# A Fourier mixer and an FFN on one core: first input by channel halves, sums before the inverse transform on GpSimd, and the first three token pairs in two passes over the weights

## The chip, the cores and the metric

One core of one Trainium2 chip. The metric is the device time of the whole program in microseconds; before the change it is 2591.12 us, the median of three runs from 2589.38 to 2592.61 us.

## What is computed

The input `x` has 8 sequences of 3008 tokens with 256 channels. Each sequence goes through a real Fourier transform over the tokens, a product with a complex filter, and the inverse transform; then a feed-forward network (FFN) is applied to every one of the 24064 tokens.

```python
X = np.fft.rfft(x, axis=1)
F = (filt_r + 1j * filt_i)[None, :, :]
y = np.fft.irfft(X * F, n=x.shape[1], axis=1).astype(np.float32)
x = y.reshape(B * S, D)
h = x @ w_in                        # 256 -> 2048
g = h * (1.0 / (1.0 + np.exp(-h)))
return (g @ w_out).astype(np.float32)   # 2048 -> 256
```

The two weight matrices arrive as 64-bit floats. The program reads them as 32-bit words and turns them into fp32 on the chip.

## The kernel before

**Order of work.** The program is written out by hand; there is no scheduler. Each engine executes its own instructions in program order, so a wait holds up everything behind it on that engine. Sequence ("batch") 0 is transformed alone, in a prologue. After that the FFN runs as 384 steps: 8 batches, 2 halves of the tokens, 3 *pairs* of token groups per half, and 8 blocks `jp` of hidden units. The transform of batch b+1 is cut into pieces that are placed between the matmuls of the FFN steps of batch b (`put(step, round, piece)`, `plan`, `plan_rest`). A step has eight rounds.

**An FFN step.** `hidden(step)` (L676) computes two 128-wide blocks of hidden units for two groups of tokens with seven matmuls in place of eight (a Strassen-Winograd scheme with weight blocks A11, A12, S3, A22, S1, S2, S4 in `w_t`). They go to three PSUM regions: `px` is used by four of them in turn, each after ScalarE has copied the value before it out (L697, L704, L710); `pyz` holds two more. VectorE adds the copies to `pyz` (L700, L711, L719) and makes the combinations of `g` (L721, `finish` L724); ScalarE applies SiLU. `project` (L735) does the seven matmuls of the step before, interleaved one by one, into the accumulators `acc`, which run over all eight `jp` of a pair. At the last one `drain` (L760) copies `acc` out, on ScalarE and VectorE by turns, and GpSimd makes seven sums (L776). `tokens(pair)` (L666) makes the combinations of a pair's inputs on VectorE before its first step.

**Weights.** There are 16 blocks j of 128 hidden units, two for each `jp`. `load_weights` brings the words, `split_weights` (L864) and `round_weights` (L890) build the exponent and the mantissa with L877, L880, L893, L895 and L899 on VectorE and L879 and L881 on ScalarE; for j = 0, 2, 4 and 6 ScalarE does L886 and L887 in place of L895. `place_weights` (L902) multiplies the two into `w_t` (L908, two instructions), and `combine_weights` (L918) makes the four Winograd sums of a `jp`. Blocks 0 to 8 are converted in the prologue, 9 to 15 in steps 0 to 6 (L1067), while the first stage of batch 1 (`stage1`, 8 pieces at round 3 of steps 0 to 7, L589) stands in the same steps.

**Prologue of batch 0.** `idle(36)` (L966) multiplies tables to warm TensorE up. `load_first` (L278) brings x in three DMAs, by tokens. `stage1_first` (L291) transforms 16 channels at a time with two matmuls each, and VectorE transposes each of the 16 results (L300). `forward(g)` (L425), for six groups g of frequencies, is the second stage. `multiply` (L441) does four VectorE instructions per group, PSUM times filter; `add` (L461) sums the products on GpSimd for g = 0 and 1 (`by_gpsimd`). For the other four groups the sums are made by TensorE, as extra terms of `inverse_first` (L482) with sign-changed tables `minus` and `neg`. `rows_first` (L502) copies the result on ScalarE and writes it to DRAM (`d2`), `load_t4` (L526) reads it back in another layout, `stage3` (L536) is the last stage and evacuates y. The conversion of blocks 2 to 8 is spread between these.

Of the kernel before, what the change touches and what calls it, by code (L numbers as in the profile page):

```python
# [46 lines left out]
FP32 = mybir.dt.float32  # L47
# [16 lines left out]
CH = 256  # L64
# [103 lines left out]
def kernel(  # L168
# [96 lines left out]
    def spectral(b):  # L265
# [12 lines left out]
        def load_first():  # L278


            view = w_t.rearrange("p j c w n -> p (j c w n)")
            for at, n0, n in ((view[:, 0:3072], 0, 12), (view[:, 3072:6144], 12, 12),
                              (x_all.rearrange("p i a n -> p (i a n)"), 24, 8)):
                nc.sync.dma_start(out=at, in_=bass.AP(tensor=x.tensor, offset=x.offset + n0 * C,
                                                      ap=[[32 * C, 128], [1, n * C]]))
            xs[0] = view[:, 0:6144].rearrange("p (n c) -> p n c", c=C)
            xs[1] = x_all.rearrange("p i a n -> p (i a n)").rearrange("p (n c) -> p n c", c=C)
            us["t2"] = view[:, 6144:14336].rearrange("p (s c) -> p s c", c=C)
            return view

        def stage1_first(k, i):  # L291

            if i == 0:
                banks[k] = bank(b, f"pa_{b}_{k}").rearrange("p a c -> p (a c)").rearrange(
                    "p (n c) -> p n c", c=16)
            n0, n = ((0, 24), (24, 8))[i]
            nc.tensor.matmul(out=banks[k][:, n0:n0 + n], lhsT=wx_t, rhs=xs[i][0:96, :, 16 * k:16 * k + 16],
                             start=True, stop=True)
            if i == 1:
                nc.vector.transpose(out=us["t2"][:, :, 16 * k:16 * k + 16].rearrange("p s c -> p c s"),  # L300
                                    in_=banks.pop(k).rearrange("p n c -> p c n"))
# [139 lines left out]
        def multiply(g, k):  # L441
            if b == 0 and g == NG - 1:

                room = raws["first"].bitcast(FP32).rearrange("p (k i r c) -> p k i r c", k=2, i=2, r=2)
                z, pt = room[:, k, 0], room[:, k, 1]
            else:
                z = zpool.tile([128, 2, C], FP32, name=f"z_{b}_{g}_{k}", tag="z")
            if b == 0 and g == NG - 1:
                pass
            elif b == 0 and k == 1:  # L450
# [9 lines left out]
        def add(g, k):  # L460
            z, pt = prods[g][k]  # L461
            eng = nc.vector if b > 0 else nc.gpsimd
# [19 lines left out]
        def inverse_first(g):  # L482
# [3 lines left out]
            pairs = prods.pop(g)  # L486
            halves[g] = ps
            for h in range(2):
                table = e_t[:, g] if h == 0 else minus[g // 4][:, g % 4]
                terms = [(table[:, :, 0], 0, 0), (table[:, :, 1], 0, 1)]  # L490
                if g not in by_gpsimd:
                    terms += [(table[:, :, 1], 1, 0), (neg[h][:, g], 1, 1)]
                for t, (lhs, which, ri) in enumerate(terms):
                    for i in range(2):
                        rows = slice(64 * i, 64 * i + 64)
                        for k in range(2):

                            nc.tensor.matmul(out=ps[i][64 * k:64 * k + 64, h, :], lhsT=lhs[rows, k],
                                             rhs=pairs[k][which][rows, ri, :], start=(h == 0 and t == 0),
                                             stop=(t == len(terms) - 1), skip_group_check=True)  # L500

        def rows_first(g):  # L502
            for i, pool, tag in ((0, qpool, "q"), (1, opool, "o")):
                qt = pool.tile([128, 2, C], FP32, name=f"q_{b}_{g}_{i}", tag=tag)
                nc.scalar.copy(out=qt, in_=halves[g][i])
                a0 = 8 * g + 4 * i
                queue = nc.gpsimd if g == NG - 2 else nc.scalar
                queue.dma_start(out=d2[a0:a0 + 4].rearrange("a n h c -> (a n) h c"), in_=qt)
# [17 lines left out]
        def load_t4(g, first=0, last=2 * NS):  # L526
# [4 lines left out]
            for h in range(2):  # L531
                queue = nc.scalar if first == 32 and h == 1 else nc.sync
# [125 lines left out]

    def combine(eng, out, in0, in1, op):
        eng.tensor_tensor(out=out, in0=in0, in1=in1, op=op)  # L660
# [5 lines left out]
    def tokens(pair):  # L666

        n, yt = pairs[pair][3], channels(pair)
        t = typool.tile([128, 4, CH], FP32, name=f"ty_{pair}", tag="ty")
# [4 lines left out]
        ty[pair] = t  # L674

    def hidden(step):  # L676

        pair, jp = divmod(step, NJP)
        n, yt, t = pairs[pair][3], channels(pair), ty[pair]
# [55 lines left out]
    def project(step):  # L735

        pair, jp = divmod(step, NJP)
        n, g = pairs[pair][3], g_t.pop(step)
        if jp == 0:
            acc[pair] = {}  # L740
        last = jp == NJP - 1

        order = PROJECT
        if jp == 0 and step in joined:
            order = PROJECT[0:2] + PROJECT[3:5] + PROJECT[2:3] + PROJECT[5:]
        elif jp == 0:
            order = PROJECT[2:3] + PROJECT[0:2] + PROJECT[3:]
        for c, k, i, h in order:
            if i not in acc[pair]:
                acc[pair][i] = accps.tile([128, 2, 256], FP32, name=f"acc_{pair}_{i}", tag=f"a{i}")  # L750

            nc.tensor.matmul(out=acc[pair][i][:, h, 0:n], lhsT=w_t[:, jp, c, 1], rhs=g[:, k, 0:n],  # L752
                             start=(jp == 0 and h == 0), stop=last, skip_group_check=True)
            if last and (h == 1 or i == 3):
                drain(pair, i)
            yield

    results = {}

    def drain(pair, i):  # L760
        n = pairs[pair][3]

        if i == 0:
            results[pair] = spool.tile([128, 8, CH], FP32, name=f"s_{pair}", tag="s")
# [3 lines left out]
        if pair == len(pairs) - 1:  # L768
            return drain_last(pair, i, n, s, acc[pair])
        copy = v.tensor_copy if i % 2 else nc.scalar.copy  # L770
        if i < 3:
            copy(out=s[:, 2 * i:2 * i + 2, 0:n], in_=acc[pair][i][:, :, 0:n])  # L772
            return
        copy(out=s[:, 6, 0:n], in_=acc.pop(pair)[3][:, 0, 0:n])
        for o, a, b in ((2, 0, 2), (5, 0, 5), (3, 5, 3), (6, 3, 6), (0, 5, 1), (4, 0, 4), (1, 3, 1)):
            combine(gp, s[:, o, 0:n], s[:, a, 0:n], s[:, b, 0:n], ALU.add)  # L776
# [363 lines left out]
```

## Time and profile before

| stretch (us) | what | PE | DVE | ACT | POOL | PE clock | DMA share |
|---|---|---|---|---|---|---|---|
| 0 to 14.4 | warm-up, first loads | 10.34 | 4.51 | 5.45 | 0.79 | 1.00 | 0.88 |
| 14.4 to 32.3 | first stage, transposes | 14.40 | 14.34 | 0.04 | 0.00 | 0.98 | 0.86 |
| 32.3 to 62.0 | filter, inverse, weights | 28.65 | 25.91 | 16.28 | 11.52 | 0.95 | 0.87 |
| 62.0 to 80.5 | weights, last stage | 15.23 | 16.52 | 10.26 | 8.22 | 0.79 | 0.81 |
| 80.5 to 151.5 | FFN steps 0 to 8 | 70.16 | 52.41 | 37.69 | 16.13 | 0.96 | 0.41 |
| 151.5 to 251.5 | FFN steps 9 to 23 | 100.00 | 66.04 | 40.76 | 13.09 | 1.00 | 0.22 |
| 251.5 to 2589 | the other steps | 2329.11 | 1511.54 | 996.42 | 376.68 | 1.00 | 0.23 |

The columns PE to POOL are busy microseconds of TensorE, VectorE, ScalarE and GpSimd in the stretch; the PE clock is the share of full speed that TensorE was granted, and the DMA share is the mean busy share of the 16 DMA engines. A busy TensorE here includes warm-up matmuls and matmuls at half clock, so its share alone doesn't say that it does useful work. A step's start is the start of its first matmul `px<-y` on TensorE.

### The profile page before, as it was taken

What the parts mean: (1) busy time and instruction counts of PE and PEld (TensorE: products, weight loads), DVE (VectorE), ACT (ScalarE), POOL (GpSimd) and SP (SyncE); (2) the same over time, 40 slices, a digit from 0 to 9 for tenths busy, and PEclk for the clock granted to TensorE, in tenths of its full rate; (3) what the DMA queues carried; (4) which work ended last, traced back from release to release, by engine and by line L of the source; (5) the groups of instructions that cost most, each with busy time, mean ns of one, the idle gap of its engine ahead of it and who ended that gap; (6) DMA issues with size and microseconds to landing.
All of it is one profiled execution on the core that took longest, in us unless ns stands there. A gap on an engine that the chain in (4) does not pass through costs nothing.

```text
span 2589.2 us, 48332 instructions
## 1 busy us (share of the span) xinstructions
PE 2567.9 (99%) x18972; PEld 2196.3 (85%) x18972; DVE 1691.3 (65%) x3569; ACT 1106.9 (43%) x3014; POOL 426.4 (16%) x672
## 2 busy tenths in 40 slices
PE   8999999999999999999999999999999999999998
PEld 6788888888888888888888888888888888888987
DVE  7766666666666766666666676666666676555554
ACT  3544444444444444443444434444444444444443
POOL 2211211121112111211122111211121112101101
PEclk9899999999999999999999999999999999999999
DMA  8431232222222222222223222231233211210000
GB/s 281 145 82 48 65 80 70 60 61 74 62 63 60 77 66 55 72 68 67 62 62 88 54 66 58 79 72 54 64 75 74 63 47 27 59 25 15 9 17 16
DMA packets 200076, 171.07 MB, mean 66 GB/s; under 512 B 122116, under 2 KB 174196, under 8 KB 199060
## 3 DMA queue, kind: packets, MB, share of 16 engines
q1 hardware_dynamic: 178520, 117.04, 18.7%
q0 software_dynamic: 16928, 44.65, 5.3%
q10 hardware_dynamic: 4400, 6.29, 0.8%
q8 instruction: 149, 2.44, 0.4%
q14 instruction: 79, 0.65, 0.1%
HBM read 96.05 MB, written 81.26 MB: 68 GB/s over the span
## 4 chain that ended last, share of the span: by engine, by line
PE 95%; DVE 1%; DMA 1%; ACT 1%; issue 0%; SPq 0%; ACTq 0%; DVEq 0%
PE acc L752 43%; PE px L689 26%; PE pyz L689 19%; PE pd L547 3%; PE pb L433 2%; PE pc L476 2%; PE pf L403 1%; PE pa L340 0%; DMA w_t<-in_x_dram 0%; DVE g L660 0%; PE pa L331 0%; DMA filt<-in_filt_i_dram 0%; ACT t L344 0%; DMA e_t<-e_tbl 0%; DVE w_t L660 0%
## 5 line engine op out<-in xcount | busy, mean ns | idle before, releaser
L752 PE MATMUL acc<-g,w_t 128*128 128x256 f32 (+1 forms) x5376 | 1512.0, 375 | 0.4 <-DVE g L660 0.4
L752 PEld LDWEIGHTS acc<-g,w_t 128*128 128x128 f32 x5376 | 1021.3, 190 | 115.7 <-DVE g L660 0.8
L660 DVE TENSOR_TENSOR g<-pyz,abc 128x256 f32<-128x256 f32 (+1 forms) x1152 | 479.7, 416 | 563.0 <-ACT abc L710 325.0
L660 DVE TENSOR_TENSOR g<-g 128x256 f32<-128x256 f32 (+3 forms) x1152 | 609.9, 529 | 196.9 <-ACT g L693 183.7
L689 PE MATMUL px<-ty,w_t 128*128 128x256 f32 (+1 forms) x2304 | 684.4, 379 | 0.5 <-ACT abc L710 0.5
L693 ACT ACTIVATE g<-g 128x256 f32<-128x256 f32 (+1 forms) x1152 | 472.9, 410 | 246.7 <-DVE g L660 246.7
L689 PEld LDWEIGHTS px<-ty,w_t 128*128 128x128 f32 x2304 | 426.3, 190 | 82.3 <-issue 26.6
L660 POOL TENSOR_TENSOR s<-s 128x256 f32<-128x256 f32 (+1 forms) x329 | 257.1, 799 | 1439.1 <-DVE s L772 1377.4
L689 PE MATMUL pyz<-y,w_t 128*128 128x256 f32 (+1 forms) x1536 | 452.9, 377 | 0.0
L689 PEld LDWEIGHTS pyz<-y,w_t 128*128 128x128 f32 x1536 | 284.3, 189 | 44.8 <-DVE g L660 5.0
L704 ACT COPY abc<-px 128x256 f32<-128x256 f32 (+1 forms) x384 | 141.5, 368 | 361.3 <-PE px L689 361.3
L710 ACT COPY abc<-px 128x256 f32<-128x256 f32 (+1 forms) x384 | 143.1, 373 | 323.7 <-PE px L689 323.7
L693 ACT ACTIVATE g<-px 128x256 f32<-128x256 f32 (+1 forms) x384 | 146.1, 381 | 308.6 <-PE px L689 308.6
L689 PE MATMUL px<-y,w_t 128*128 128x256 f32 (+1 forms) x768 | 230.2, 381 | 1.1 <-ACT y L246 1.0
L689 PE MATMUL pyz<-ty,w_t 128*128 128x256 f32 (+1 forms) x768 | 225.7, 376 | 0.2 <-DVE g L660 0.2
L689 PEld LDWEIGHTS px<-y,w_t 128*128 128x128 f32 x768 | 141.9, 189 | 23.6 <-issue 5.9
L689 PEld LDWEIGHTS pyz<-ty,w_t 128*128 128x128 f32 x768 | 145.9, 190 | 17.4 <-DVE g L660 1.0
L697 ACT COPY abc<-px 128x256 f32<-128x256 f32 (+1 forms) x384 | 135.5, 353 | 19.5 <-PE px L689 19.5
L547 PEld LDWEIGHTS pd<-wi_t,t 48*64 48x64 f32 x4096 | 69.3, 139 | 32.0 <-ACT g L693 16.4
L547 PE MATMUL pd<-wi_t,t 48*64 48x47 f32 x4096 | 77.2, 238 | 2.3 <-DMA t<-d 1.9
L415 POOL DMA_DIRECT2D d<-tf x144 | 71.4, 503 | 24.0 <-DVE tf L411 20.4
L772 ACT COPY s<-acc 128x512 f32<-128x512 f32 (+1 forms) x94 | 54.3, 578 | 47.5 <-PE acc L752 47.5
(114 smaller groups left out, 1309.1 us busy)
## 6 DMA issues: line engine op xcount, KB each, us to landing
t<-d SPq DMA_DIRECT2D x120, 192.0 KB
d<-q POOLq DMA_DIRECT2D x86, 256.0 KB, 2.6
t<-d SPq DMA_DIRECT2D x84, 256.0 KB
out_dram<-o SPq DMA_DIRECT2D x636, 32.0 KB
d<-tf POOLq DMA_DIRECT2D x144, 96.0 KB, 3.0
xr<-in_x_dram SPq DMA_DIRECT2D x6, 1472.0 KB
x_all<-in_x_dram SPq DMA_DIRECT2D x72, 96.0 KB
x_all<-xr SPq DMA_DIRECT2D x72, 96.0 KB
```

What stands on the lines that cost most here:

```text
L415: nc.gpsimd.dma_start(out=d1[k // 2, :, k % 2, n0:n0 + 4], in_=us["tf"][32 * k:32 * k + NS].rearrange("p q n c -> p (q n) c"))
L433: nc.tensor.matmul(out=ps[k][32 * j:32 * j + 32, ri, :], lhsT=d_t[rows, 4 * g + at, ri, :], rhs=t2[rows, at, :], start=True, stop=True)
L476: nc.tensor.matmul(out=ps[j][64 * k:64 * k + 64, a, :], lhsT=e_t[rows, g + a, k, ri, :], rhs=zs[k][rows, ri, :], start=(a == 0 and ri == 0 ...
L547: nc.tensor.matmul(out=ps[h][c0:c0 + 64, cb, i, :], lhsT=t4s[g][rows, i, 128 * cb + c0:128 * cb + c0 + 64], rhs=wi_t[rows, :], start=True, ...
L660: eng.tensor_tensor(out=out, in0=in0, in1=in1, op=op)
L689: nc.tensor.matmul(out=out, lhsT=w_t[:, jp, c, 0], rhs=rhs, start=start, stop=True, skip_group_check=True)
L693: nc.scalar.activation(out=g[:, k, 0:n], in_=g[:, k, 0:n] if src is None else src, func=AFT.Silu)
L697: nc.scalar.copy(out=sums[:, 0, 0:n], in_=xo)
L704: nc.scalar.copy(out=sums[:, 1, 0:n], in_=xo)
L710: nc.scalar.copy(out=sums[:, 2, 0:n], in_=xo)
L752: nc.tensor.matmul(out=acc[pair][i][:, h, 0:n], lhsT=w_t[:, jp, c, 1], rhs=g[:, k, 0:n], start=(jp == 0 and h == 0), stop=last, skip_group ...
L772: copy(out=s[:, 2 * i:2 * i + 2, 0:n], in_=acc[pair][i][:, :, 0:n])
```

## The change

It has five parts. (1) x of batch 0 comes as channels 0 to 127 in one DMA and channels 128 to 255 in two, on 96 partitions, in runs of 128 channels; the first eight transposes need the first DMA alone. (2) All sums before the inverse transform are made by GpSimd, except those of the second half of groups 4 and 5, which VectorE makes; the extra terms on TensorE and the `neg` tables are gone. (3) Only blocks 0 to 3 are converted before the FFN, blocks 1 to 3 after the inverse transform. Blocks 4 to 15 are converted in steps 0 to 3 and 5 to 12, and their Winograd sums are made by GpSimd. (4) So that the FFN can start with four blocks, pair 0 runs over `jp` 0 and 1, pairs 1 and 2 over `jp` 0 to 3, and each takes the rest later: six runs in the place of three, with three more `tokens`, three more drains and a partial sum that GpSimd adds. (5) Some queues change: `load_t4` of the last rows of groups 2 and 3 goes to ScalarE's queue, and several buffers are used for other things.

```diff
-            for at, n0, n in ((view[:, 0:3072], 0, 12), (view[:, 3072:6144], 12, 12),
-                              (x_all.rearrange("p i a n -> p (i a n)"), 24, 8)):
-                nc.sync.dma_start(out=at, in_=bass.AP(tensor=x.tensor, offset=x.offset + n0 * C,
-                                                      ap=[[32 * C, 128], [1, n * C]]))
+            for at, n0, n, c0 in ((view[:, 0:4096], 0, 32, 0), (view[:, 4096:6144], 0, 16, 128),
+                                  (x_all.rearrange("p i a n -> p (i a n)"), 16, 16, 128)):
+                at = at.rearrange("p (n c) -> p n c", c=128)
+                nc.sync.dma_start(out=at[0:96], in_=bass.AP(tensor=x.tensor, offset=x.offset + n0 * C + c0,
+                                                            ap=[[32 * C, 96], [C, n], [1, 128]]))
...
-            eng = nc.vector if b > 0 else nc.gpsimd
+            eng = nc.vector if b > 0 or (g > 3 and k == 1) else nc.gpsimd
...
-                if g not in by_gpsimd:
-                    terms += [(table[:, :, 1], 1, 0), (neg[h][:, g], 1, 1)]
...
-                nc.scalar.copy(out=qt, in_=halves[g][i])
+                copy = nc.vector.tensor_copy if (g, i) == (NG - 1, 1) else nc.scalar.copy
+                copy(out=qt, in_=halves[g][i])
...
-                queue = nc.scalar if first == 32 and h == 1 else nc.sync
+                queue = nc.scalar if first == 32 and g > 1 else nc.sync
...
+    runs = [(0, 0, 2), (1, 0, 4), (2, 0, 4), (0, 2, 8), (1, 4, 8), (2, 4, 8)]
+    runs += [(pair, 0, NJP) for pair in range(3, len(pairs))]
+    schedule = [(run, jp) for run, (_, first, end) in enumerate(runs) for jp in range(first, end)]
...
+        kept = partial.pop(pair, None)
+        if end < NJP:
+
+            room = x_all[:, pair - 1] if pair else upool.tile([128, 2, 512], FP32, name="partial", tag="u")
+            partial[pair] = room.rearrange("p a (i n) -> p (a i) n", n=CH)
         for o, a, b in ((2, 0, 2), (5, 0, 5), (3, 5, 3), (6, 3, 6), (0, 5, 1), (4, 0, 4), (1, 3, 1)):
...
+        if kept is not None:
+            for k, o in enumerate(FINAL):
+                combine(gp, s[:, o, 0:n], s[:, o, 0:n], kept[:, k, 0:n], ALU.add)
...
+    for g in range(4):
         part["forward"](g)
     for g in range(NG):
         for k in range(2):
             part["multiply"](g, k)
+            part["add"](g, k)
+        if g == 3:
+            part["forward"](5)
+        if g > 0:
+            inverse(g - 1)
+        if g == 1:
+            part["forward"](4)
...
+    inverse(NG - 1)
     for later in range(4):
+        part["load_t4"](later, 32, 2 * NS)
+    split(1)
+    rounded(1)
+    placed(1)
     combine_weights(0)
+    split(2, 3)
+    rounded(2, 3)
+    placed(2, 3, eng=gp)
+    combine_weights(1, eng=gp)
+    weights(6, 7)
+    idle(24)
     for g in range(4):
         part["stage3"](g)
...
-    for j in range(9, NJ):
-        put(j - 9, 1, lambda j=j: (split(j), rounded(j)))
-        put(j - 9, 5, placed, j)
+    for j in range(4, NJ):
+        at = j - 4 if j < 8 else j - 3
+        put(at, 1, lambda j=j: (split(j), rounded(j)))
+        put(at, 5, placed, j)
         if j % 2:
-            put(*((j - 8, 5) if j < 15 else (j - 9, 6)), combine_weights, j // 2, 0)
-            put(*{13: (j - 8, 7), 15: (j - 8, 1)}.get(j, (j - 7, 5)), combine_weights, j // 2, 1)
+            put(at + 1, 1, lambda jp=j // 2: combine_weights(jp, eng=gp))
...
+    begun = ((-2, 1), (0, 5), (4, 5), (8, 5), (14, 5), (18, 5))
...
+        step, rnd = begun[run] if pair < 3 else combines[pair % per]
+        pending.append((pair // per * STEPS + step + rnd / ROUNDS, 98, lambda run=run: tokens(run)))
```

## The prediction

> **What bounds the kernel now.** I read the page first: its busy shares, then its chain of work that ended last.
>
> ```profile
> PE 2567.9 (99%) x18972; PEld 2196.3 (85%) x18972; DVE 1691.3 (65%) x3569; ACT 1106.9 (43%) x3014; POOL 426.4 (16%) x672
> PE 95%; DVE 1%; DMA 1%; ACT 1%; issue 0%; SPq 0%; ACTq 0%; DVEq 0%
> ```
>
> TensorE sets the end, and the change leaves the FFN's matmuls as they are. So only two things can move the time: when FFN step 0 starts, and how long TensorE stalls in the steps whose VectorE and ScalarE work changes. The timeline of the prologue (start, duration, engine and line):
>
> ```profile
> 3.60 10.31 PE L964 MATMUL idle<-wx_t 96*128 96x128 f32 x72 [3.60 <-DMA wx_t<-wx_tbl]
> 17.95 14.25 DVE L300 STREAM_TRANSPOSE w_t<-pa 128x512 f32<-128x512 f32 x16 [7.25 <-PE pa L297]
> 34.33 0.69 DVE L455 TENSOR_TENSOR z<-pb,filt 128x512 f32<-128x512 f32 x1 [0.89 <-PE pb L433]
> 61.95 7.86 PE L964 MATMUL idle<-wx_t 96*128 96x128 f32 x68
> 72.10 6.76 PE L547 MATMUL pd<-wi_t,t 48*64 48x47 f32 x246 [1.89 <-DMA t<-d]
> 80.54 1.19 PE L689 MATMUL px<-y,w_t 128*128 128x256 f32 x2 [0.98 <-ACT y L246]
> ```
>
> Transposes run from 17.95 to 32.2, the filter products start at 34.33, the inverse ends at 61.95, the last stage at 79.6, and step 0 starts at 80.54. Then the timeline of a step that converts a block (the step that starts at 105.08), with one line from a later step without conversion:
>
> ```profile
> 107.98 0.42 DVE L877 TENSOR_SCALAR e<-raw 128x512 uint32<-128x512 uint32 x1
> 108.43 0.72 ACT L879 ACTIVATE e<-e,bias_t 128x512 f32<-128x512 uint32 x1 [1.96 <-DVE e L877]
> 109.06 0.61 ACT L881 ACTIVATE m<-m 128x512 f32<-128x512 uint32 x1
> 109.58 0.35 ACT L704 COPY abc<-px 128x256 f32<-128x256 f32 x1
> 109.71 0.69 DVE L893 SCALAR_TENSOR_TENSOR m<-raw,m 128x512 f32<-128x512 uint32 x1 [0.97 <-ACT m L881]
> 111.52 0.42 DVE L660 TENSOR_TENSOR g<-pyz,abc 128x256 f32<-128x256 f32 x1
> ...
> 147.82 0.37 ACT L704 COPY abc<-px 128x256 f32<-128x256 f32 x1 [0.94 <-PE px L689]
> ```
>
> The `px` copy L704 comes 4.50 us after the step's start, behind L879 and L881; in the step that starts at 145.39 without a conversion it comes after 2.43 us. TensorE doesn't feel it, because the first stage of batch 1 (four matmuls, 1.72 us) stands just there. Such steps last 7.84 to 7.97 us; 14 matmuls of 0.4315 us and 1.72 make 7.76.
>
> **What the skill says.** The Trainium skill, "SBUF — State Buffer", section "Who interferes with whom": a VectorE instruction with two SBUF inputs, or in a two-port mode, and a GpSimd instruction that reads SBUF exclude each other; one with a PSUM input doesn't. The trace agrees:
>
> ```profile
> 63.46 3.44 POOL L660 TENSOR_TENSOR w_t<-w_t 128x256 f32<-128x256 f32 x4 [0.47 <-DVE w_t L908]
> 63.63 0.95 DVE L880 TENSOR_SCALAR scratch<-raw 128x512 uint32<-128x512 uint32 x1
> 72.55 0.96 DVE L895 TENSOR_SCALAR e<-e 128x512 uint32<-128x512 f32 x1
> 74.68 1.71 DVE L908 TENSOR_TENSOR w_t<-m,e 128x256 f32<-128x256 f32 x2
> 153.55 1.49 DVE L660 TENSOR_TENSOR g<-g 128x256 f32<-128x256 f32 x2
> ```
>
> Beside GpSimd L880 takes 0.95 us for 0.42, L908 1.71 for 0.75, `finish` 1.49 for 0.87; L899 took 1.11 for 0.69; the products from PSUM stay at 0.68. "TensorE: Matmul & The Clock Gate", section "What's actually happening", says that about 3.4 us of idling halve the clock; the trace has 0.50 from about 73 to 86 us although TensorE waited just 1.9 us, so I assume half clock at the same place after. "DMA: Bandwidth & Descriptors", section "Specifications", gives 512 bytes as the least for line rate; the packets of 512 bytes in the trace have a median of 27 ns, 303 GB/s over 16 engines, against 460 ns for 12288 bytes (427 GB/s).
>
> **The prologue after.** *First input.* The first DMA has 3072 packets: 3072 x 27 ns / 16 = 5.2 us. With block 0 (some 1.5 us) and a start at 3.0 it lands near 10.5, the other two near 13 and 16. But `idle(36)` holds TensorE until 13.9, so the first result comes at 14.8, and transposes run from 15.0 to 29.2: 3.0 us are won, not seven. At twice the packet time the DMAs land near 15, 20 and 25.5; the last eight transposes (7.1 us) then end at 33.5, 1.3 us later than before. Filter products start at 34.33 - 3.0 = 31.3.
>
> *Filter and inverse.* VectorE has 24 products of 0.60 us without conversions between: 14.4 us. The GpSimd sums take 0.69 each (35.77 to 40.56), 2.75 per group against 2.4 for VectorE, and trail without holding it; buffers are free in time. VectorE's own four sums read SBUF beside GpSimd: 4 x 0.95 less overlap, some 3.5. The last sum is done at 49.2, the last inverse (1.9 us, as at 41.09 to 43.0) at 51.3: 10.6 us before 61.95.
>
> *Last stage.* Copy 0.6, two issues, 2.3 us from issue to the reader's start (50.36 to 52.72): rows are in DRAM near 55.5. Synchronous queue: 8 + 8 + 2 issues of 0.42 and one of 0.34 from 48.2 end at 56.1, with gaps 56.5; with 2.5 us to land (69.28 to 72.10 before, less the issue) `stage3` starts at 59.0 and, at 7.1 us as before, ends at 66.1. *Weights.* ScalarE is in order, and its four `load_t4` issues wait for those rows: until 57.2 nothing behind them runs, and L879 of block 1 is behind them. From there L879 and L881 1.25, L893 to L899 1.6, L908 0.75, sums of `jp` 0 1.5, four L877/L880 1.4, ScalarE's share of blocks 2 and 3 3.7, then its five y copies of 0.8: 57.2 + 14.2 with 1.0 of overlap = 70.4. This is later than TensorE's 66.1 + 1.2, so step 0 starts at 70.4: **-10.1 us** (bounds 67.5 and 73.5).
>
> **The FFN after.** Ideal step lengths are the same; I add stalls.
>
> *Conversions without the first stage beside them.* Blocks 11 to 15 fall in steps 8 to 12. There L704 still comes after about 4.65 us, so the fifth `px` matmul starts at 5.1, not 3.45: +1.65 us each in steps 8 and 9. In 10 and 11 `stage3` (1.26 us) fills most of it, but its y copies add 0.8; in 12 `forward` leaves 0.4: 1.65 x 2 + 0.8 x 2 + 0.4 = **5.3**.
>
> *GpSimd beside conversions.* The drains of the three first runs put seven sums (5.5 to 5.95 us) into steps 3, 7 and 11, which convert. `finish` (+0.6), L877, L880, L895 (+0.53 each) and L893, L899 (+0.42 each) give 3.0; 0.5 vanishes in the 0.97 us wait for L881. I take 2.0 each, bounds 1.0 and 2.5. Behind these wait L704, the fifth `px` matmul and all after it. Sums of `jp` 2 and 5 (2.9 to 3.9 us) cover `finish` in steps 2 and 9: 0.5 each. **7.0**, bounds 3 and 9.
>
> *More `tokens`.* 1.46 us each at round 5 of steps 0 and 8, ahead of L719 and the next step's `finish` and L877: the free time there is 1.1 to 1.4, L908 takes 0.75 of it: 1.3 + 1.1; the first `tokens`, beside GpSimd's sums of `jp` 1, +1.0: **3.4**. In step 4 it is hidden, as nothing is converted.
>
> *Drains and the rest.* ScalarE's copy of 0.59 before the next `px` copy: 0.45 in each of steps 2, 6 and 10; steps 13 to 18 +0.7; block 6 needs L886 and L887 on ScalarE, +1.3 in step 2: **3.4**. GpSimd's 12 sums of the partial results are read a step later: 0.
>
> *Removed.* The stalls of steps 1 to 7 before (7.84 + 7.89 + 7.85 + 7.97 + 7.85 + 8.65 + 7.98 by the starts of `px<-y`, less 7 x 7.76) are 1.7, 0.2 in step 8: **-1.9**.
>
> Sum: 5.3 + 7.0 + 3.4 + 3.4 - 1.9 = +17.2; with -10.1 it is +7.1, and 2591.1 + 7.1 = **2598 us**.
>
> **Rivals.** *A, no change:* the two engines' exclusion costs 3, `tokens` and drains half: 5.3 + 3 + 1.7 + 1.7 - 1.9 = 9.8 against -10.1: 2591. For it: most VectorE work of a step reads PSUM. Against: a conversion doesn't. *B, faster:* step 0 at 67.5 (TensorE's limit, if rows land earlier than under the load seen at 58 to 62) and stalls of 6, as if only the missing first stage counted: 2591 - 13 + 6 = 2584. For it: in the step at 105.19 VectorE is busy 6.25 of 7.86 us, so there is room on average; against: the order, not the busy time, sets L704. *C, first input late:* at 54 ns a packet transposes end 1.3 us later than before instead of 3.0 earlier, and tables and filters, which ScalarE issues after the second DMA has landed, some 2 us later still: 2598 + 6 = 2604. For it: packets of 1024 bytes rise from a median of 46 ns to 71 when two queues press on the engines at 28 to 32 us; against: at 3 to 16 us the DMA moves 415 GB/s.
>
> **How the numbers follow.** Forecast 0.47 (0.02 of it within 0.2%), A 0.20, B 0.23, C 0.10. The bound of 0.2% is 5.2 us: slower 0.45 + 0.10 = 0.55, same 0.22, faster 0.23. The low end, 2583, takes in the better half of B; with stalls at their bounds the forecast reaches 2591 to 2604, and part of C goes to 2606.
>
> **What would show it.** First transpose at 15.0; products of the last group end near 47; last inverse ends near 51; step 0 at 70.4, with ScalarE's L879 of block 1 behind its `load_t4` issues. Steps 8 and 9 at 7.7 us or more instead of 6.1; steps 3, 7 and 11 at least 1.5 us over their ideal. I am wrong if L879 of block 1 runs before the rows have landed, if step 0 comes before 68, or if steps 3 and 7 last under 8.3 us.

## The result and the profile after

The changed kernel takes 2617.45 us (2617.03 to 2618.9, 4 runs) against 2591.76 (2589.38 to 2592.61) for the kernel before in the same comparison: a ratio of 1.010, 95% interval 1.0085 to 1.0114, slower. The forecast was 2598 us, at most 2606. The direction was right, the size was not: +27.1 us between the two profiled spans (2616.3 and 2589.2) instead of +7.1.

The page of the kernel after, busy shares and chain of work that ended last:

```profile
PE 2564.7 (98%) x18792; PEld 2188.3 (84%) x18792; DVE 1708.9 (65%) x3573; ACT 1107.3 (42%) x3017; POOL 475.7 (18%) x732
PE 93%; DVE 3%; DMA 2%; ACT 1%; issue 1%; SPq 0%; ACTq 0%; DVEq 0%
```

TensorE's part of the chain falls from 95 to 93%, VectorE's rises from 1 to 3 and the DMA's from 1 to 2; GpSimd works 49 us more. So the places to look are the DMA in the prologue and VectorE in the FFN steps.

The timeline of the prologue after (start, duration, engine and line):

```profile
3.88 10.49 PEld L975 LDWEIGHTS idle<-wx_t 96*128 96x128 f32 x72 [3.88 <-DMA wx_t<-wx_tbl]
16.15 7.07 DVE L299 STREAM_TRANSPOSE w_t<-pa 128x512 f32<-128x512 f32 x8 [7.18 <-PE pa L297]
18.93 0.19 ACT L985 COPY warm<-w_t 96x1 f32<-96x1 f32 x1 [10.67 <-DMA w_t<-in_x_dram]
23.78 7.09 DVE L299 STREAM_TRANSPOSE w_t<-pa 128x512 f32<-128x512 f32 x8 [0.56 <-PE pa L297]
32.10 0.69 DVE L453 TENSOR_TENSOR z<-pb,filt 128x512 f32<-128x512 f32 x1 [0.67 <-PE pb L432]
38.54 1.76 ACT L995 ACTIVATE minus<-e_t,bias_t 128x1024 f32<-128x1024 f32 x2 [19.42 <-DMA filt<-in_filt_r_dram]
41.42 0.69 DVE L453 TENSOR_TENSOR room<-pb,filt 128x512 f32<-128x512 f32 x1 [4.45 <-DMA filt<-in_filt_i_dram]
67.58 0.72 ACT L890 ACTIVATE scratch<-scratch,bias_t 128x512 f32<-128x512 uint32 x1 [8.56 <-DMA t<-d]
72.32 7.39 PE L542 MATMUL pd<-wi_t,t 48*64 48x47 f32 x256 [11.06 <-DMA t<-d]
80.68 0.76 PE L691 MATMUL px<-y,w_t 128*128 128x256 f32 x1 [0.97 <-ACT y L246]
```

FFN step 0 starts at 80.68 us, where it started at 80.54 before: the prologue won nothing, though it converts four weight blocks instead of nine. The second DMA of the input has landed only at 18.93 (14.25 before), and with it everything that ScalarE issues behind it is late: `minus` at 38.54, a filter product that waits 4.45 us for its filter. L890 of block 1 (the prediction's L879) sits behind the `load_t4` issues as forecast, but until 67.6 us, not 57.2.

The timeline of FFN step 9 after (it converts block 12):

```profile
164.22 3.65 POOL L660 TENSOR_TENSOR w_t<-w_t 128x256 f32<-128x256 f32 x4 [7.20 <-DVE w_t L919]
165.82 1.47 DVE L660 TENSOR_TENSOR g<-g 128x240 f32<-128x240 f32 x2
167.21 0.94 DVE L888 TENSOR_SCALAR e<-raw 128x512 uint32<-128x512 uint32 x1
168.19 0.72 ACT L890 ACTIVATE e<-e,bias_t 128x512 f32<-128x512 uint32 x1 [3.05 <-DVE e L888]
168.82 0.61 ACT L892 ACTIVATE m<-m 128x512 f32<-128x512 uint32 x1
169.34 0.34 ACT L706 COPY abc<-px 128x240 f32<-128x240 f32 x1
169.73 1.17 PE L691 MATMUL px<-ty,w_t 128*128 128x240 f32 x2 [2.52 <-ACT abc L706]
170.69 1.81 PE L755 MATMUL acc<-g,w_t 128*128 128x240 f32 x4
```

Read it from the top: GpSimd's four Winograd sums of `jp` 5 run from 164.22 to 167.87. Beside them `finish` takes 1.47 us and L888 0.94 instead of 0.42. ScalarE's L890 waits for L888, L706 stands behind L890 and L892, and TensorE waits 2.52 us for L706. The last two lines are new: after the wait two matmuls take 1.17 us where they take 0.57 otherwise, because the granted clock there is 0.50. Such a step before had no wait of TensorE for L706 at all.

By the starts of `px<-y`, steps 0 to 23 take 197.3 us after and 170.9 before, 26.4 more. From step 24 on the two traces differ by 0.6 us in 2338. So the prologue gave 0.1 us, these FFN steps 26.4 and the rest 0.6.

### The profile page after: what moved, and what is told of

Same layout as the page of the kernel before. It is cut to its first block, busy times and chain, and to the rows that moved or that the text cites. A ratio compares the mean times of both kernels' runs of the same rounds, so it can differ in the third digit from the quotient of the medians.

```text
span 2616.3 us, 48075 instructions
## 1 busy us (share of the span) xinstructions
PE 2564.7 (98%) x18792; PEld 2188.3 (84%) x18792; DVE 1708.9 (65%) x3573; ACT 1107.3 (42%) x3017; POOL 475.7 (18%) x732
## 3 DMA queue, kind: packets, MB, share of 16 engines
q1 hardware_dynamic: 184280, 115.99, 18.7%
## 4 chain that ended last, share of the span: by engine, by line
PE 93%; DVE 3%; DMA 2%; ACT 1%; issue 1%; SPq 0%; ACTq 0%; DVEq 0%
PE acc L755 42%; PE px L691 25%; PE pyz L691 18%; PE pd L542 3%; PE pb L432 2%; PE pc L474 2%; DVE g L660 1%; PE pf L402 1%; DMA w_t<-in_x_dram 1%; DMA d<-q 1%; PE pa L339 0%; DMA t<-d 0%; DMA d_t<-d_tbl 0%; DVE e L888 0%; DVE ty L660 0%
## 5 line engine op out<-in xcount | busy, mean ns | idle before, releaser
L660 DVE TENSOR_TENSOR g<-g 128x256 f32<-128x256 f32 (+3 forms) x1152 | 616.6, 535 | 196.8 <-ACT g L695 183.6
L691 PE MATMUL px<-ty,w_t 128*128 128x256 f32 (+1 forms) x2304 | 686.7, 380 | 13.3 <-ACT abc L706 11.3
L660 POOL TENSOR_TENSOR s<-s 128x256 f32<-128x256 f32 (+1 forms) x338 | 264.8, 800 | 1427.5 <-DVE s L777 1372.6
L706 ACT COPY abc<-px 128x256 f32<-128x256 f32 (+1 forms) x384 | 141.4, 368 | 356.5 <-PE px L691 356.5
```

Source lines behind the costliest of these rows:

```text
L691: nc.tensor.matmul(out=out, lhsT=w_t[:, jp, c, 0], rhs=rhs, start=start, stop=True, skip_group_check=True)
L706: nc.scalar.copy(out=sums[:, 1, 0:n], in_=xo)
```

## The experiments

All kernels are the kernel after with the edit shown, unless said otherwise. FFN step 0 at 80.68 us and the step lengths of the kernel after are the yardstick: steps 2, 3, 7, 9 and 11 take 12.15, 9.68, 10.69, 11.06 and 11.77 us, 55.4 together.

### First input: packet size or partitions?

`x_tokens128` reads the first input again by tokens, `x_tokens96` does so into the 96 partitions that are used:

```diff
-  for at, n0, n, c0 in (... two channel halves, [[32 * C, 96], [C, n], [1, 128]])
+  for at, n0, n in ((view[:, 0:3072], 0, 12), (view[:, 3072:6144], 12, 12), (x_all..., 24, 8)):
+      nc.sync.dma_start(out=at[0:P], in_=... ap=[[32 * C, P], [1, n * C]])      # P = 128 or 96
   # (stage1_first is that of the kernel before)
```

> The kernel after, with the first input read as in the kernel before (three DMAs by tokens on 128 partitions, packets of 12288 bytes instead of 512). Theory T1: the 512-byte packets (46 ns each, some 200 GB/s) hold the DMA engines until about 22 us and push filters, tables and weight loads back into the time of the d2 writes. Then here the last transposes end at 32 us as before, minus is made at 33 instead of 38.5, the last inverse ends at 51 to 53 instead of 55.6, and FFN step 0 starts at 71 to 75 instead of 80.7; time 2608 to 2612 us. Rival R1: the loads of weight blocks 1 to 5 and ScalarE's load_t4 issues ahead of block 1's L890 set the start, whatever the first input does: step 0 at 78 or later, 2615 us or more.

> As x_tokens128, but only the 96 partitions that hold data (packets of 12288 bytes). If the size of the packets is what slowed the input (T1), the DMA rate of the first 14 us is 340 GB/s or more as with 128 partitions, and the first transposes come at 17 us or earlier. If it is the number of partitions (rival), the rate stays below 260 GB/s, and the first transpose comes no earlier than with 128 partitions.

`x_tokens128`: 2612.2 us (ratio to before 1.0085, 1.0068 to 1.0101). `minus` comes at 32.9 us as expected, but step 0 only at 77.1: between the two theories. The first input explains 3.5 us of the prologue, and something else the rest. `x_tokens96` (2615.9 us, one run; step 0 at 80.06) gains next to nothing, although its packets are as long. Busy time by stretch of the first 14.4 us (the last three columns are TensorE's granted clock, the DMA engines' busy share and GB/s); first the kernel after, then `x_tokens128`, then `x_tokens96`:

```profile
0.00:14.40 14.40, 10.52 (x72) 10.49 (x72) 2.21 (x5) 4.06 (x6) 0.79 (x15) 1.00 0.93 190
```

```profile
0.00:14.40 14.40, 10.58 (x64) 10.58 (x65) 2.21 (x5) 4.25 (x7) 0.79 (x15) 1.00 0.87 341
```

```profile
0.00:14.40 14.40, 10.46 (x62) 10.46 (x63) 2.21 (x5) 4.06 (x6) 0.80 (x15) 1.00 0.88 228
```

The DMA engines are about as busy in all three (0.87 to 0.93) and move 190, 341 and 228 GB/s. With packets of 12288 bytes in both, a packet into 128 partitions takes 460 ns (median) and one into 96 partitions 833: T1, which blamed the size of the packets alone, falls. That called for the converse, halves into 128 partitions:

```diff
-  nc.sync.dma_start(out=at[0:96], in_=... ap=[[32 * C, 96], [C, n], [1, 128]])
+  nc.sync.dma_start(out=at, in_=... ap=[[32 * C, 128], [C, n], [1, 128]])
```

> The kernel after, its first input by channel halves as it is (packets of 512 bytes) but on all 128 partitions instead of 96, the last 32 of them data that nothing reads. Theory P, after x_tokens96: what halves the rate of the first input is that only 96 partitions are written, not the packets of 512 bytes. Then the first 14.4 us move 320 GB/s or more (190 in the kernel after), a 512-byte packet takes 27 to 32 ns (46), the copy to warm comes by 14.5 us (18.9), the transposes end by 30 us, and step 0 starts at 75 to 77.5 us: 2611 to 2614 us. Theory S (packet size): under 260 GB/s, packets at 40 ns or more, the copy at 17 us or later, step 0 at 79.5 or later, 2616 us or more.

```profile
0.00:14.40 14.40, 10.50 (x70) 10.50 (x71) 2.21 (x5) 4.06 (x6) 0.79 (x15) 1.00 0.90 246
```

2616.75 us (ratio 1.0100, 1.0083 to 1.0117), step 0 at 80.4. The packet falls from 46 to 32 ns, as theory P said, but the rate is 246 GB/s and the copy to `warm` comes at 17.75, as theory S said. Either one spoils it: 96 partitions (236 GB/s of packets of 12288 bytes) or runs of 512 bytes (16 x 512 / 32 ns = 256 GB/s); together they give 16 x 512 / 46 = 178. Only long runs into 128 partitions reach 427. A quarter of what goes into 128 partitions is not needed, which takes back most of the gain: the second DMA of `halves128` has landed just 1.2 us earlier than that of the kernel after (17.75 against 18.93). Why 96 partitions halve the rate I did not find out.

### What else held the prologue

`h128_both` is `halves128` with two more edits:

```diff
-  if g == 3:  for later in range(4): part["load_t4"](later, 0, 24)
-  if g == 4:  for later in range(4): part["load_t4"](later, 24, 32)
+  if g == 4:  for later in range(4): part["load_t4"](later, 0, 32)
-  queue = nc.scalar if first == 32 and g > 1 else nc.sync
+  queue = nc.gpsimd if first == 32 and g > 1 else nc.sync
```

> halves128 with two more edits: the loads of rows 0 to 24 and 24 to 32 for the last stage made one (16 issues instead of 24), and the four load_t4 issues of ScalarE moved to GpSimd's queue, so that L890 of block 1 is not behind them. Theory Q (an issue waits for the landing of the DMA eight issues earlier, whose completion semaphore it takes over; in the kernel after these waits hold the synchronous queue for 6.0 us, and ScalarE is held 8.6 us): L890 of block 1 runs by 57 us, stage3 starts by 66 us (72.3 in the kernel after), step 0 by 74.5. Rival: the transfers of the rows themselves (DMA engines busy) set the last landing, stage3 starts at 67.5 or later and step 0 at 75.5 or later.

The waits of the synchronous engine's DMA queue from 45 to 76 us (engine and line, who released it: us in total, times, longest), kernel after and `h128_both`:

```profile
SPq L528 <- DMA t<-d: 6.0, 4, 2.2
SPq L528 <- DMA d<-q: 4.9, 1, 4.9
```

```profile
SPq L528 <- DMA d<-q: 11.3, 3, 8.9
SPq L528 <- DMA t<-d: 0.4, 1, 0.4
```

In the kernel after, issues of `load_t4` wait 6.0 us for other `load_t4` transfers (6.6 in `halves128`), which no data needs: they go to other partitions. In the semaphore events of the trace the DMAs of the two hardware queues take eight completion semaphores in turn, and an issue that takes one over waits for the DMA that had it. With eight issues fewer this wait is 0.4 us. L890 of block 1 comes at 61.1 instead of 66.4, `stage3` at 67.5 instead of 72.1 and step 0 at 76.2 instead of 80.4. Each edge of theory Q was missed, by 1.5 to 4.1 us, and the rival's are met (67.5 and 75.5): the last rows themselves need 4.5 us to land, and the synchronous queue now waits 11.3 us for rows. The gain of 4.3 us is there (2610.19 us, one run). Which of the two edits brought how much of it, these runs don't separate.

Then both repairs at once, without and with more idle matmuls to keep TensorE's clock up (`x128_t4`: the tokens of `x_tokens128` and these two edits; `x128_warm`: also `idle(52)` for `idle(24)`):

> The kernel after with the first input by tokens on 128 partitions (x_tokens128), rows 0 to 32 loaded in one load and four load_t4 issues on GpSimd's queue (as h128_both), and idle(52) instead of idle(24), so that TensorE has work until the last stage's rows land. Theory: without the 7 to 11 us of waiting TensorE keeps its full clock; stage3 starts by 65.5 us and lasts under 5.5 us instead of 7.1 to 7.5, step 0 starts by 71.5 at full clock (9.0 to 9.5 us long so far, 8.3 or less then), time 2606 us or less. Rival: the weight chain behind L890 of block 1 (14.2 us) sets step 0 at 73.5 or later whatever TensorE's clock, time 2608.5 or more.

> x128_warm with idle(24) as in the kernel after. If the issues brought the gain (an issue waits for the landing of the one eight issues earlier), stage3 starts by 65.5 us as in x128_warm, lasts 7 us or more at half clock, and step 0 starts at 73 to 74.5 us. If the idle matmuls brought it, step 0 starts at 76 us or later.

The timeline of `x128_t4`:

```profile
56.09 0.72 ACT L891 ACTIVATE scratch<-scratch,bias_t 128x512 f32<-128x512 uint32 x1 [0.98 <-DVE scratch L892]
63.36 7.21 PE L543 MATMUL pd<-wi_t,t 48*64 48x47 f32 x254 [0.29 <-DMA t<-d]
71.55 1.19 PE L692 MATMUL px<-y,w_t 128*128 128x256 f32 x2 [0.98 <-ACT y L246]
```

Step 0 starts at 71.55 us, 9.1 earlier than in the kernel after, and earlier than I had expected (2605.57 us, one run). Block 1 is converted at 56 us, before the rows have landed. The idle matmuls of `x128_warm` do what they should (the granted clock is 1.00 from 55 to 70 us and most of `stage3` takes 4.1 us), but `stage3` starts 1.5 us later behind them and then waits, and step 0 comes at 71.99: no gain (2607.54 us; ratio 1.0059, 1.0043 to 1.0074). So the two edits of the issues brought the gain, and not the idle matmuls.

The same idea in the kernel before, `idle(42)` for `idle(34)`:

> The kernel before with idle(42) instead of idle(34): eight more idle matmuls of 0.46 us a pair of passes cover the 1.89 us in which TensorE waits for the last rows ahead of stage3. Theory W (a wait of about 2 us is what halves the clock, as in steps 2 and 9 of the kernel after): stage3 runs at full clock and takes 4 to 5 us instead of 6.8, step 0 (8.8 us) is 0.7 us or more shorter, time 2586 to 2589 us. Rival: the clock falls there for another reason and stays at 0.5 until 86 us; the time is that of the kernel before within 0.05%, or up to 0.5 us later.

2590.72 us, ratio 0.9998 (0.999 to 1.0006): no change. The clock stays at 1.00 until 74 us and 0.98 until 78 and step 0 is 0.74 us shorter, but `stage3` has to wait for its rows and y copies in between, and step 0 starts 0.2 us earlier only. Theory W is right on the clock and wrong on the time, which can't be told from no change.

### GpSimd's sums and the conversions

```diff
 # sums_vec
-  put(at + 1, 1, lambda jp=j // 2: combine_weights(jp, eng=gp))
+  put(at, 5, combine_weights, j // 2, 0)
+  put(at + 1, 5, combine_weights, j // 2, 1)
 # no_partial: in drain
+  if end == NJP or o == 2:
       combine(gp, out, s[:, a, 0:n], s[:, b, 0:n], ALU.add)
-  for k, o in enumerate(FINAL):
+  for k, o in enumerate(FINAL[:1]):
```

> The kernel after, with the Winograd sums of jp 2 to 7 on VectorE, half of them in the step that places the block and half in the next, instead of GpSimd. Theory T2: GpSimd's sums beside the conversions' VectorE instructions (they exclude each other) make TensorE wait in steps 2, 7, 9 and 11, and the half clock after these waits doubles the damage. Then steps 2, 7, 9 and 11, now 12.2, 10.7, 11.1 and 11.8 us, fall by 2 to 3.5 us each, and the time is 2606 to 2610 us. Rival R2: the conversions' ScalarE and VectorE work ahead of the px copy, with no first stage beside it, costs this whichever engine sums: steps 9 and 11 stay above 10 us, 2613 us or more.

> The kernel after, without six of the seven GpSimd sums in the drains of the first three runs and without three of the four additions of partial results in the drains of the next three: these sums are left out, so the output is not the reference's. T2: steps 3 and 7 (9.7 and 10.7 us) fall by 1.5 to 2 us, step 11 (11.8) by 1 to 2, the time by 4 to 6 us to 2611 to 2613. R2: each of the three falls by less than 0.7 us, the time by 2 us at most.

> sums_vec and no_partial together: Winograd sums of jp 2 to 7 on VectorE, and most of GpSimd's sums in the drains of the first six runs left out, so the output is not the reference's. No GpSimd work then stands beside the conversions. T2 (the two engines' exclusion): steps 2, 3, 7, 9 and 11 together, 55.4 us in the kernel after and 55.8 in sums_vec, fall to 45 or less (each 8.3 to 9.5), time 2607 to 2610 us. R2 (the conversions themselves, with no first stage beside them): steps 9 and 11 stay above 9.5 and the five above 48 us, time 2612 or more.

`sums_vec`: 2621.03 us (1.0119, 1.0104 to 1.0135), slower than the kernel after; T2's time is missed, and R2's is met with step 9 below its edge. Steps 2 and 9 fall by 2.2 and 1.7 us, of which 1.3 and 1.5 are the clock ("The same wait, two clocks"), but step 3 rises by 2.9 and step 7 by 1.6. The timeline of its step 3:

```profile
110.19 2.93 DVE L919 TENSOR_TENSOR w_t<-m,e 128x256 f32<-128x256 f32 x2
110.56 0.73 POOL L660 TENSOR_TENSOR partial<-s 128x256 f32<-128x256 f32 x1
111.25 1.60 POOL L660 TENSOR_TENSOR s<-s 128x256 f32<-128x256 f32 x2
113.84 0.70 PE L691 MATMUL pyz<-y,w_t 128*128 128x256 f32 x2 [2.81 <-DVE g L660]
```

VectorE is now later, and so L919 meets the drain's sums on GpSimd: its two instructions take 2.93 us instead of 0.75, and TensorE waits 2.81. `no_partial` leaves those sums out: steps 3, 7 and 11 fall by 1.5, 1.1 and 1.8 us (2614.03 us, one run), nearly what T2 asked for. (Step 2 falls by 1.3, but it falls as much in `halves128`, whose FFN is that of the kernel after: this is the clock, not the edit.) With both edits, `sums_vec_np`, the five steps take 48.6 us (2614.46, one run): the gain is large, but R2's 48 is right too. VectorE's own sums are still in that number, so the next two runs take each cause away and put only DMAs in its place:

```diff
 # no_gp: as no_partial, and
-  put(at + 1, 1, lambda jp=j // 2: combine_weights(jp, eng=gp))
+  put(at + 1, 1, fake_sums, j // 2)          # DMA from x into the sums' places
 # no_conv
-  put(at, 1, lambda j=j: (split(j), rounded(j)))
-  put(at, 5, placed, j)
+  put(at, 1, fake, j)                        # DMA from x into the block's places
```

> The kernel after with GpSimd's work beside the FFN conversions left out and nothing put in its place: the Winograd sums of jp 2 to 7 (their places in w_t are filled by DMA with values of x) and most sums in the drains of the first six runs; the output is not the reference's. Theory E (the exclusion of VectorE by GpSimd, and the half clock after the waits that it makes): steps 2, 3, 7, 9 and 11, 55.4 us together in the kernel after, fall to 46 or less. Theory C (the chain of a conversion over VectorE and ScalarE is itself too long for a step that has no first stage or has drains and tokens beside it): they stay at 48 or more.

> The kernel after with the conversions of blocks 4 to 15 left out of the FFN (their places in w_t are filled by DMA with values of x), GpSimd's sums, the drains and tokens all kept; the output is not the reference's. Theory C: without conversions steps 1 to 13, 121.4 us in the kernel after, come within 4 us of their ideal (about 94), whatever GpSimd does, and the time is 2594 or less. Theory E: GpSimd's sums still hold up finish, g and y copies: steps 1 to 13 stay 7 us or more above the ideal, and the time is 2599 or more.

Steps 1 to 13 take 118.6 us in the kernel after (the 121.4 in the expectation was mis-added), 106.3 in `no_gp` and 95.9 in `no_conv`; the prediction's ideal lengths sum to 94.1 (steps 6 to 9 are short ones now, with 240 tokens to a group in place of 256). The time is 2606.99 and 2596.14 us (one run each; step 0 starts 1.8 and 2.1 us later in them). TensorE's waits from the start of step 0 to that of step 14, in the kernel after, `no_gp` and `no_conv`:

```profile
PE px L691 <- ACT abc L706: 11.3, 9, 2.5
PE pyz L691 <- DVE g L660: 4.7, 6, 1.5
PE px L691 <- ACT abc L712: 1.9, 4, 0.9
```

```profile
PE px L691 <- ACT abc L706: 4.7, 7, 1.4
PE pyz L691 <- DVE g L660: 2.6, 4, 0.9
```

```profile
PE pyz L691 <- DVE g L660: 0.9, 1, 0.9
PE px L691 <- ACT abc L712: 0.5, 1, 0.5
```

Theory E is shown: without GpSimd the five steps fall from 55.4 to 43.1 us, no wait is longer than 1.4 us, and the clock is 1.00 in steps 1 to 13. What E expected of `no_conv` was not borne out: without conversions GpSimd's sums, drains and tokens cost 1.8 us together, as C had it. So GpSimd's work costs next to nothing alone; 12.3 us (118.6 - 106.3) come from the two side by side, and 10.4 (106.3 - 95.9) from the conversions without GpSimd. A rival is left: the missing sums could help because something waited for their results or their buffers. Steps 1 to 13 by stretch, in the kernel after and in `no_gp` (stretch, its length, busy time and count of PE, PEld, DVE, ACT and POOL, then granted clock, DMA share, GB/s), speak for the exclusion:

```profile
90.20:208.76 118.56, 102.47 (x584) 77.25 (x585) 90.31 (x178) 55.88 (x138) 53.98 (x76) 0.97 0.34 97
91.64:197.93 106.29, 98.40 (x584) 75.51 (x585) 77.72 (x178) 55.45 (x138) 17.20 (x34) 1.00 0.47 131
```

VectorE executes 178 instructions in both, and they are busy for 90.31 us beside GpSimd and 77.72 without it: the instructions themselves are 12.6 us longer, which waiting for results would not make them. In step 9 of `no_gp` the same instructions as above:

```profile
160.39 0.84 DVE L660 TENSOR_TENSOR g<-g 128x240 f32<-128x240 f32 x2
161.15 0.42 DVE L889 TENSOR_SCALAR e<-raw 128x512 uint32<-128x512 uint32 x1
161.60 0.72 ACT L891 ACTIVATE e<-e,bias_t 128x512 f32<-128x512 uint32 x1 [1.89 <-DVE e L889]
162.75 0.34 ACT L706 COPY abc<-px 128x240 f32<-128x240 f32 x1
```

`finish` is back at 0.84 and L889 (L888) at 0.42; step 9 takes 8.42 us.

### When in the step

```diff
 # split_r4
-  put(at, 1, lambda j=j: (split(j), rounded(j)))
+  put(at, 4, lambda j=j: (split(j), rounded(j)))
 # x128_warm_r4 (x128_warm and:)
-  put(at + 1, 1, lambda jp=j // 2: combine_weights(jp, eng=gp))
+  put(at + 1, 4, lambda jp=j // 2: combine_weights(jp, eng=gp))
+  # the sums of the first three drains: in round 4 of the step after the drain
```

> The kernel after, with each FFN conversion's first instructions three rounds later in its step (round 4 instead of 1), so that the px copies L706 and L712 stand ahead of the conversion's two ScalarE instructions in ScalarE's queue. R2 (TensorE waits for L706, which is queued behind L890 and L892): the waits of 2.06 and 2.52 us for L706 in steps 2 and 9 go, steps 2, 9 and 11 fall by 1.5 to 3 us each, with no half clock after them, time 2608 to 2612 us. T2 alone (VectorE is late because GpSimd excludes it, whatever the order): the wait moves to the next VectorE result (g or the later px copy), the three steps fall by less than 1 us each, 2615 us or more.

> x128_warm (2607.5 us) with GpSimd's sums beside the conversions three to five rounds later in their step: the Winograd sums of jp 2 to 7 in round 4 instead of 1, the sums of the first three drains in round 4 of the step after the drain instead of at once. Nothing is left out. Theory L: what costs is GpSimd's exclusion of L888 to L910, on which L706 and TensorE wait in the first half of a step; in the second half VectorE's instructions mostly read PSUM. Then steps 2, 3, 7, 9 and 11, 55.4 us together in x128_warm, fall to 49 or less, time 2598 to 2602 us. Rival M: GpSimd then holds up L919, the g differences and the next step's finish as much: the five stay above 53 us, time 2605 or more.

`split_r4` takes 2654.02 us (1.0243, 1.0228 to 1.0258), 37 more than the kernel after. The waits for L706 are gone, but TensorE waits 15.3 us for the `silu` behind L890 and L892 and 22.4 us for `g` from VectorE, up to 3.1 us at a time, and the clock is below 1.00 in eight of steps 1 to 13. R2's remedy falls, and T2's edges are met: the wait has moved to other results of VectorE and ScalarE. A conversion is a chain between VectorE and ScalarE of some 3.5 us to L910, and round 1, ahead of the first stage's four matmuls, is the better of the two places tried: in the steps that have a first stage TensorE has something else to do there.

`x128_warm_r4`: 2607.24 us (1.0062, 1.0045 to 1.0078), as `x128_warm`. The five steps fall to 48.7 us as theory L said, but step 5 rises by 1.5 and step 8 from 7.28 to 11.26, where the moved drain sums meet the next conversion. In time, M is right: the collision was moved, not removed. No version here beats the kernel before.

### The same wait, two clocks

Two windows of the kernel after, its steps 2 and 9, and then of `halves128`, whose FFN is the same program (stretch, its length, busy time and count of PE, PEld, DVE, ACT and POOL, then granted clock, DMA share, GB/s):

```profile
99.05:111.20 12.15, 9.61 (x33) 6.85 (x32) 7.56 (x14) 6.75 (x16) 6.55 (x11) 0.86 0.33 89
162.67:173.73 11.06, 7.68 (x29) 6.27 (x29) 8.16 (x17) 3.47 (x10) 4.00 (x5) 0.85 0.24 66
```

```profile
98.35:109.19 10.84, 8.30 (x34) 5.91 (x32) 6.87 (x13) 6.73 (x16) 5.25 (x9) 1.00 0.30 84
161.18:170.76 9.58, 6.21 (x29) 5.15 (x29) 8.07 (x17) 3.46 (x10) 4.00 (x5) 1.00 0.16 33
```

TensorE waits the same 2.1 us (step 2) and 2.5 us (step 9) for L706 in both. In the kernel after the clock is halved for 3.41 us behind each of these waits, in `halves128` it is not: 1.3 and 1.5 us of difference. The Trainium skill, "TensorE: Matmul & The Clock Gate", section "What's actually happening", has the clock fall after an idle window of about 3.4 us that runs freely, whatever the kernel does. The traces agree: in the clock records of all runs, every stretch of full or of half clock but the last of the trace lasts a multiple of 3.41 us. On this grid, the window of the wait in step 2 and the next one, in the kernel after and then in `halves128` (columns as above):

```profile
104.47:107.88 3.41, 1.44 (x6) 1.06 (x6) 1.38 (x2) 3.38 (x8) 0.00 (x0) 1.00 0.44 115
107.88:111.30 3.42, 2.94 (x8) 2.28 (x8) 2.12 (x5) 1.73 (x5) 2.58 (x5) 0.50 0.33 79
```

```profile
101.51:104.92 3.41, 2.18 (x7) 0.81 (x5) 2.32 (x4) 2.06 (x4) 1.00 (x2) 1.00 0.15 16
104.92:108.34 3.42, 2.11 (x9) 1.56 (x10) 1.26 (x3) 3.30 (x8) 0.52 (x1) 1.00 0.28 99
```

In the kernel after the wait lies in one window, in which TensorE is busy for 1.44 us, and the next runs at half clock. In `halves128` it lies across two, with 2.18 and 2.11 us of work, and the clock stays. So a window need not be idle from end to end: in steps 2 and 9 of the seven traces with this FFN the clock fell after windows with 1.17 to 1.49 us of work and stayed after those with 1.47 or more. Where the windows lie against the program differs from execution to execution.

## Why the prediction was wrong

The 19.5 us between forecast and time are 10.3 in the prologue and 9.2 in the FFN.

*What bounds the kernel.* Right: all but 0.6 us came from the start of step 0 and from TensorE's stalls in the first 24 steps.

*First input (the failed step of the prologue).* "3072 x 27 ns / 16 = 5.2 us" took the packet time from a DMA of 96 packets. The first input's packets took 46 ns, and its three DMAs landed at 15.0, 18.9 and 23.0 instead of 10.5, 13 and 16. (The sum for the first, 3.0 + 1.5 + 5.2, makes 9.7 and not 10.5; nothing hung on it, because the idle matmuls held TensorE until later.) Transposes end at 30.9, not 29.2, which is little; what I had put down to rival C alone, that tables and filters follow late, came with it: `minus` at 38.5 and 4.5 us of waiting for a filter, so that the last inverse ends at 55.6 instead of 51.3. Undone, step 0 comes 3.5 us earlier. The Trainium skill, "DMA: Bandwidth & Descriptors", section "Specifications", which I leaned on for 512 bytes as the least for line rate, is not borne out here: 256 GB/s at 512 bytes into 128 partitions, 427 at 12288. Its section "Rules for kernel authors" names 128 partitions for the most bandwidth, and that the runs do show (460 against 833 ns).

*Last stage and weights.* "8 + 8 + 2 issues of 0.42 ... end at 56.1" counted the issues and not what they wait for: data, and the landing of the DMA that had the same completion semaphore. The writes of the rows took 2.3 to 7.1 us from issue to landing, the last two 3.5 and 3.8, where I had taken 2.3 for all. The last row landed at 65.1, 9.5 us after the last inverse and not 4.2, and L890 of block 1 ran at 67.6 instead of 57.2: 4.3 us of the difference are the late inverse, some 6 the rows and the issues behind them. From there to step 0 it is 13.1 us, and I had said 13.2: the mechanism, block 1 behind ScalarE's `load_t4` issues, was right. That `x128_t4` starts step 0 at 71.55, 1.1 us from the forecast 70.4, is chance: its input is that of the kernel before, and its block 1 runs at 56.1, ahead of the rows.

*GpSimd beside conversions (the failed term of the FFN).* 7.0 us, bounds 3 to 9, measured 12.3. Of this 2.3 is half clock behind the waits of steps 2 and 9, for which the prediction had no term: `halves128`, with full clock, takes 116.3 us for steps 1 to 13 (2.8 less in these two, 0.5 more in step 3). The rest, 10.0, is above the upper bound. `halves128` less `no_gp` gives it by steps: 2.1, 2.8 and 2.8 in steps 3, 7 and 11, priced at 2.0 each, and 1.2 each in steps 2 and 9, priced at 0.5 for `finish` alone. There GpSimd's sums held L888 as well (0.94 us in step 9), and with it L890, L706 and TensorE. The section "Who interferes with whom" of the Trainium skill's "SBUF — State Buffer" describes this exclusion, and the durations above agree.

*Conversions, tokens and drains.* 5.3 + 3.4 + 3.4 = 12.1; measured, as what `no_gp` is above the ideal in steps 1 to 13, 12.2 (0.7 of the forecast was meant for steps 13 to 18). Step 9 was 8.42 there, step 8 7.26 where I had asked for 7.7. Right as a sum.

*What was left out.* Steps 14 to 23 take 69.2 us against 64.7; 1.5 of that only moves four short steps to 6 to 9, so 3.0 are stalls, where I had 0.7. Step 0 is 0.7 longer. *Removed:* 1.9 forecast, 1.8 measured. The sum: 12.3 + 12.2 + 3.0 + 0.7 - 1.8 = 26.4.

*Rivals and range.* C, given 0.10, was right that tables and filters come late, but its packets of 54 ns and its transposes that end at 33.5 did not come, and even it (2604) had only 6 us for it. Both upper bounds together, 73.5 and 9 us, give 2603, inside the range that ended at 2606: the bounds themselves were too narrow. All three signs of being wrong that I had named look for a kernel faster than forecast; none of them came.

## What to carry to other kernels

Take a transfer's rate from one of the same size, run length and number of partitions; and when loads get late, follow what else is issued behind them and how many DMAs are in flight, since an issue can wait for a transfer that has nothing to do with it. Work moved to GpSimd is free only where VectorE at that time reads PSUM or nothing waits for it: look at what VectorE does in that very part of the step, and expect the collision to move, not to vanish, when either side is shifted. A chain between VectorE and ScalarE belongs where TensorE has matmuls that don't depend on it, and waits of 2 us cost more than their length, because the clock may fall behind them, if they lie badly in its windows of 3.41 us.

## What the hardware showed that I had not expected

- 12288-byte packets into 96 partitions take 833 ns, into 128 partitions 460: three quarters of the bytes arrive no sooner than all.
- Packets of 512 bytes took 46 ns (96 partitions) and 32 (128), against 27 ns in a short DMA of 96 packets.
- Behind the first input's DMA of 3072 such packets, the issue of the next, with 1536, held the synchronous queue for 6.67 us; one of 128 long packets took 0.43.
- TensorE's clock changed only on a grid of 3.41 us. Waits of 2.1 and 2.5 us, shorter than one window, halved it in some executions of the same FFN and not in others, by where they lay in the windows. In `split_r4` half clock accounts for at most 18.7 us of steps 1 to 13 (each step's length times what its granted clock lacks of 1, summed).
- Two VectorE products of 0.75 us together took 2.93 beside GpSimd's sums: the engine was shut out for nearly three of GpSimd's instructions.
